# Sparse attention feeding a squared-ReLU layer: the second batch's loads ahead of w_out, first loads by head pair, free PSUM banks, and vector work that yields

## The chip, the cores and the metric

The kernel runs on one core of a Trainium2 chip. A core has five engines with an instruction stream each: TensorE (PE in the profile: matmuls and transposes), VectorE (DVE), ScalarE (ACT), GpSimd (POOL) and SyncE (SP). GpSimd and SyncE also issue the transfers between the device's memory (HBM) and the on-chip buffer (SBUF). Matmul results stand in eight PSUM banks. The metric is the device time of one execution in microseconds (us), as the median over the runs.

## The reference

The inputs q, k and v have 8 batches of 8 heads, 576 positions and 64 dimensions, in fp32. The weights are w_in (512 x 2048) and w_out (2048 x 512).

```
scores = q @ k.T / 8
mask   = heads 0-3: 0 <= i - j < 32          ("local")
         heads 4-7: j <= i and i % 32 == j % 32   ("strided")
attn   = softmax(where(mask, scores, -1e9)) @ v
x      = attn with the heads side by side: 4608 rows of 512
h      = x @ w_in
out    = (s * max(h, 0)**2 + b) @ w_out
```

## The kernel before

**Attention.** A batch is cut into four pairs of heads, m = 0 to 3: two local pairs and two strided ones. q, k and v are loaded and turned to fp16 by the transfer itself (GpSimd's queue), except that the first batch's local v is staged in fp32 by SyncE in the room of w_out (`vl_stage`) and cast by GpSimd. A pair's work (`pair_steps`) is a list of small TensorE steps: transposes of q and k (L405 in the first two batches, L413 after), scores (L533; in the first batch preceded by a matmul that adds the mask, L530), weighted sums with v (L590) and transposes of the result x (L638). Between the steps stand ScalarE's exponentials (L551), VectorE's masks (L559), reciprocals (L605) and scalings (L616), and copies out of PSUM that ScalarE or VectorE may take (L317). The result is xT, the input of the dense layers. In later batches some of the transposes are done by transfers on SyncE's queue.

**Dense layers.** x is cut into nine blocks T of 512 rows. For each block, `ff1` makes 16 x 4 matmuls with w_in (L883), which ScalarE clips at zero (L910; VectorE at L912 for block 0), and a square of two results at a time (L918 on ScalarE, L920 on VectorE) gives gT. For blocks 0 to 2, `ff2` makes 4 x 16 matmuls with w_out (L941), evicted by VectorE (L952). For blocks 3 to 8, `ff2_seven` makes seven products in place of eight from sums of parts of gT (`sums_post`, L723 on VectorE) and of w_out (w_mix), with matmuls at L851 and evictions at L770, L782. The bias needs sums over w_out, made in `bcs_steps` (L968, L979) early in block 0's second layer.

**Order of the work.** Nothing is reordered at run time: each engine runs its stream in order, and waits where an operand isn't there. The streams are written by a planner (`Plan`) when the kernel is built. It keeps a clock `t`, due times `done` for every piece of data, and times `free` for the engines. TensorE's steps are taken from the attention lists or from f1 and f2 as they come due; work of the other engines is posted with `post` (what it needs, its cost by engine, the function that writes it) and written by `flush`, the piece that became ready first being first, on the engine that the plan says ends it first. A step that opens a PSUM bank names a `Group`: a tag (t, s, a, f1 or f2) with one or two banks, taken in strict rotation, so that a step is due only when the bank used `bufs` groups ago was given back. `group_of` chooses the tag by kind and batch, in a fixed rotation over tags for the first batches. While TensorE has nothing due at the start, `keep_running` writes matmuls on constants (L1177).

**Loads.** `load_qk`, `load_s`, `early_v`, `load_vl`, `load_w_in` and `load_w_out` issue on GpSimd, in this order: q, k, strided q, strided k and strided v of batch 0; w_in in three pieces (`weights_in`, after strided q has landed); then `second`. Local q and k have lines ql and kl in the profile, strided ones qs and ks, and v is v_loc and vs. Due times for transfers are figures in the code (`arrive`, `landing`). The core of `second`:

```
weights_out(range(1))
fetch_qk(1)
weights_out(range(1, 4))
load_vl(1)
...
early_v(1)
```

Of the kernel before, what the change touches and what calls it, by code (L numbers as in the profile page):

```python
# [15 lines left out]
class Plan:  # L16
# [6 lines left out]

    LAT = {"A": 70.0, "V": 70.0, "P": 70.0, "D": 12000.0, "X": 7000.0, "Y": 12000.0}

    def __init__(self):
        self.t = 0.0
        self.done = {}
        self.pend = []
        self.free = {"A": 0.0, "V": 0.0, "P": 7000.0, "D": 0.0, "X": 0.0, "Y": 0.0}  # L30
        self.count = {}

    def ready_at(self, needs):
        if any(k not in self.done for k in needs):
# [6 lines left out]
    def flush(self):  # L41
        while True:
            best = None
            for p in self.pend:
                r = self.ready_at(p[0])
                if r is not None and r <= self.t and (best is None or r < best[0]):
                    best = (r, p)
            if best is None:
                return
            r, p = best  # L50
            self.pend.remove(p)
            eng = min(p[1], key=lambda e: max(self.free[e], r) + p[1][e])
            end = max(self.free[eng], r) + p[1][eng]
            self.free[eng] = end
            p[2](eng)
            for k in p[3]:
                if isinstance(k, Group):
                    k = ("rel", k.tag, k.n)
                soon = isinstance(k, tuple) and k[0] == "soon"
                self.done[k] = end + (6000.0 if soon else p[4] or self.LAT[eng])  # L60

    def step_ready(self, s):
        r = self.ready_at(s.needs)
        if r is None:
            return None
        if s.group is not None:
            n = self.count.get(s.group.tag, 0)
            if n >= s.group.bufs:
                k = ("rel", s.group.tag, n - s.group.bufs)
                if k not in self.done:  # L70
                    return None
                r = max(r, self.done[k])
        return r

    def emit(self, s):
        if s.group is not None:
            s.group.n = self.count.get(s.group.tag, 0)
            self.count[s.group.tag] = s.group.n + 1
        s.fn()
        self.t += s.ns  # L80
        for k in s.keys:
            self.done[k] = self.t + 200.0
        for p in s.posts:
            self.post(*p)
        if s.after is not None:
            s.after()

    def next_time(self):

        nxt = [v for v in self.done.values() if v > self.t]  # L90
        assert nxt, "nothing left that could make a step ready"
        return min(nxt)

# [4 lines left out]
class Group:  # L98


    def __init__(self, tag, bufs):
        self.tag, self.bufs, self.n = tag, bufs, None


class Step:
# [6 lines left out]
def kernel(  # L112
# [11 lines left out]
    nc = tc.nc  # L124
# [118 lines left out]
    stage_v(range(2))  # L243
    nc.sync.dma_start(out=negs, in_=h_neg.ap())
    nc.vector.memset(ones16, 1.0)
    nc.vector.memset(part32, 1.0 / 32)
    nc.vector.memset(vl_stage[0:LPAD], 0.0)
    for i in range(2):
        nc.vector.memset(qD_loc[i], 0.0)
        nc.vector.memset(kT_loc[i][:, 0:LPAD], 0.0)  # L250
        nc.vector.memset(qD_str[i], 0.0)
    for i in range(NV):
        nc.vector.memset(v_loc[i][:, :, :, D:D + 1], 1.0)
# [4 lines left out]
    for tl in p_bufs[False]:  # L258
        nc.vector.memset(tl[:, 16 * SQ:], 0.0)

    loaded = {}
    paired = {}

    def load_qk(b):
        for name, src in (("q", q), ("k", k)):
            tl = inp.tile([LQ, NL], FP16, tag=name + "l", name=name + "l")
            loaded[b, name + "l"] = tl
            if b >= (QB_DMA if name == "q" else KB_DMA):

                dst = tl.rearrange("p (m t e d) -> p m e t d", m=2, t=LT, e=2)  # L270
                for h in range(4):
                    nc.gpsimd.dma_start(out=dst[:, h // 2, h % 2],
                                        in_=src[b, h].rearrange("(t p) d -> p t d", p=LQ))
            else:
                nc.gpsimd.dma_start(out=h4(tl), in_=view_l(src, b))
        for name, src in (("q", q), ("k", k)):
            if name == "k":
                ts = ks[b % 2]
            elif b < QS_DMA + 2:
                ts = inp.tile([SR, NS], FP16, tag="qs", name="qs")  # L280
            else:
                ts = loaded[b - 2, "qs"]
            if name == "k" and b in (2, 3) or name == "q" and b in (QS_DMA, QS_DMA + 1):
                nc.gpsimd.memset(ts[64:SR], 0.0)
            load_s(ts, src, b)
            loaded[b, name + "s"] = ts
# [47 lines left out]
    def cast_v(b, loc, mm, key):  # L334
        nt, np_, dst = (LT, 128, v_loc) if loc else (ST, SQ, v_str)

        def g(eng):
            src = vl_stage if loc else loaded[b, "vs"].rearrange(
                "p (h t d) -> p h t d", h=4, d=D)
            for h in range(2 * mm, 2 * mm + 2):  # L340
                copy_on(eng, out=dst[b % NV][0:np_, h, :, 0:D], in_=src[:, h])
        n = nt * D
        plan.post([key], {"P": 1000.0} if loc else {"A": 2 * (170 + 0.83 * n), "V": 540.0}, g,
                  [("cast", b, mm) if loc else ("in", "vs", b, mm)])
        if loc:
            rows_before(b, mm, ("cast", b, mm))

    def rows_before(b, mm, key):
# [5 lines left out]
        def g(eng):  # L354
# [4 lines left out]
    TB, SB, AB, F1B, F2B = 1, 2, 1, 2, 2  # L359
    HEAD_T = 2  # L360
    PE_MASK = 1
    ps = {tag: [psum.tile([128, PS], FP32, name=f"ps_{tag}{i}") for i in range(n)]
          for tag, n in (("t", TB), ("s", SB), ("a", AB), ("f1", F1B), ("f2", F2B))}

    taken = {"a": 0, "t": 0, "s": 0}

    def group_of(kind, b, m, q=False):

        t, a, f1, f2 = ("t", TB), ("a", AB), ("f1", F1B), ("f2", F2B)
        banks = {"a": [a], "t": [t], "s": [("s", SB)]}[kind]  # L370
        if b == 0:
            banks = {"a": [f2, f2, f1], "t": [t, a], "s": [("s", SB), ("s", SB), f1]}[kind]
        elif b == 1 and kind == "a":
            banks = [f1, f1, a]
        elif b >= KB_DMA and kind == "a":
            banks = [a, t]
        elif b == 1 and q:
            banks = [t, f2]
        taken[kind] += 1
        return Group(*banks[taken[kind] % len(banks)])  # L380

    def bank(group):
        return ps[group.tag][group.n % group.bufs]

    def pair_steps(b, m):

# [196 lines left out]
        def av(e, j, group):  # L583
# [13 lines left out]
            if j % per == per - 1:  # L597
# [2 lines left out]
                j0 = j - per + 1  # L600

                def rc(eng):
                    st["rec", e, j] = recp.tile([128, 6, 1], FP32, tag="rec" + group.tag,
                                                bufs=group.bufs, name="rec")
                    nc.vector.reciprocal(out=st["rec", e, j][0:nq, 0:per],  # L605
                                         in_=st["pa", e, j][0:nq, 0:per, D:D + 1])

# [445 lines left out]
    load_qk(0)  # L1053
    early_v(0)
    plan.free["P"] = 7100.0
    for name, at in (("q", 6950.0), ("k", 8750.0)):
        arrive(both(name + "l", 0), at)
    arrive(both("qs", 0), 10100.0)
    arrive(both("ks", 0), 11600.0)
    plan.done["raw", "v", False, 0] = 13800.0  # L1060
    after_landing(0, loaded[0, "ql"][0:1, 0:1])
    stage_v(range(2, 4))
    nc.sync.dma_start(out=masks, in_=h_mask.ap())
    nc.sync.dma_start(out=s_sb, in_=moe_s.to_broadcast([128, 1]))
# [7 lines left out]
        for keys, cost in ([0], 2700), ([1], 2500), ([2, 3], 5000):  # L1072
            arrive([("w_in", c) for c in keys], landing(cost))

    for mm, at in (0, 7100.0), (1, 14400.0):
        plan.done["raw", "v", True, 0, mm] = at
        cast_v(0, True, mm, ("raw", "v", True, 0, mm))
    plan.post([("in", "vl", 0, 0)], {"P": 3300.0}, weights_in, [("w",)])

    def weights_out(chunks):  # L1080
        load_w_out(chunks)
# [2 lines left out]

    def second(eng):

        weights_out(range(1))
        fetch_qk(1)
        weights_out(range(1, 4))
        load_vl(1)  # L1090
        plan.done["raw", "vl", 1] = landing(3200)
        for mm in range(2):
            rows_before(1, mm, ("raw", "vl", 1))
        early_v(1)

    plan.post(both("vl", 0) + both("vs", 0) + [("w",)], {"P": 14000.0}, second, [("free",)])

# [29 lines left out]
    for T in range(NBLK):  # L1127
        if T == 0:

            gr = [Group(*x) for x in (("s", SB), ("s", SB), ("f1", F1B), ("f1", F1B))]  # L1130
            cts = FIRST
            f1 += [ff1(T, ft, ct, gr[ft], cts, True) for ct in cts for ft in range(4)]
        for ft in ff_order(T)[0 if T else 4:]:
            gr = Group("f2", F2B) if T == 0 and ft % 4 < 2 else Group("f1", F1B)
            for ct in range(4):
                f1.append(ff1(T, ft, ct, gr))
        if T == 0:
# [24 lines left out]
    def keep_running(until):  # L1162

        ghz = 1.2 if plan.t < 6000 else 2.4
        n = min(int((until - 100.0 - plan.t) * ghz) - 20, 512) // 128
        for tag, bufs in (("f1", F1B), ("s", SB), ("f2", F2B)):
            k = ("rel", tag, plan.count.get(tag, 0) - bufs)
            if k[2] < 0 or plan.done.get(k, until) <= plan.t:
                break
        else:  # L1170
            return False
        if n < 1:
            return False
        out = ps[tag][plan.count.get(tag, 0) % bufs][:, 0:128 * n]

        def f():
            nc.tensor.matmul(  # L1177
# [90 lines left out]
```

## Time and profile before

| | |
|---|---|
| median of 8 runs (lowest to highest) | 308.95 us (307.92 to 309.71) |
| profiled execution: its time, its span | 307.92 us, 306.1 us |
| TensorE, weight loads | 297.1 us busy (97%), 206.4 us |
| VectorE, ScalarE, GpSimd | 215.9 (71%), 183.5 (60%), 93.2 us (30%) |
| transfers | 37.31 MB, 122 GB/s in the mean |
| granted TensorE clock | 0.998 |

The span runs from the first to the last event of the profiled execution; its own time has 1.8 us more around it. Busy time of an engine is the time in which one of its recorded instructions was running; waits inside a stream are listed apart, with what ended them. A table by stretches gives, for each stretch of time, each engine's busy time with the number of instructions that ran in it (x), then the granted clock, the transfer share and GB/s.

### The profile page before, as it was taken

How to read it: one execution, taken by the hardware profiler on the slowest of the kernel's cores; microseconds unless marked ns; L12 is line 12 of the kernel's file. 1: busy time of each engine (PE TensorE's matmuls, PEld its weight loads, DVE VectorE, ACT ScalarE, POOL GpSimd, SP SyncE). 2: the span in 40 equal slices, each digit the busy share in tenths (PEclk: the TensorE clock that was granted, in tenths of full speed). 3: DMA queues.
4: the chain of work that ended last, by engine and by line, in shares of the span. 5: the costliest groups of instructions: out<-in, count | busy, mean ns of one | idle time of the engine just before them, and what ended most of it. 6: DMA issues, size and time to landing. Idle time of an engine off the chain costs nothing.

```text
span 306.1 us, 6880 instructions
## 1 busy us (share of the span) xinstructions
PE 297.1 (97%) x2686; PEld 206.4 (67%) x2686; DVE 215.9 (71%) x479; ACT 183.5 (60%) x330; POOL 93.2 (30%) x136
## 2 busy tenths in 40 slices
PE   8898999999999999999999999999999999999995
PEld 3764655666655567777567776778888666766884
DVE  6665767799868678449897987688765366737563
ACT  2875856698957795668287945794525444444300
POOL 8561539910880581079105840000000000000000
PEclk9999999999999999999999999999999999999999
DMA  7999999999999999899997999714010200300223
GB/s 128 183 209 207 213 164 169 201 187 149 78 138 184 110 150 109 177 152 135 137 194 132 142 149 188 167 26 133 2 36 35 71 1 34 105 0 2 82 74 121
DMA packets 100796, 37.31 MB, mean 122 GB/s; under 512 B 80875, under 2 KB 97771, under 8 KB 100763
## 3 DMA queue, kind: packets, MB, share of 16 engines
q0 software_dynamic: 57200, 18.08, 59.8%
q1 hardware_dynamic: 43562, 18.78, 31.9%
q8 instruction: 21, 0.34, 0.5%
q14 instruction: 13, 0.10, 0.1%
HBM read 36.86 MB, written 10.32 MB: 154 GB/s over the span
## 4 chain that ended last, share of the span: by engine, by line
PE 87%; DMA 9%; POOL 1%; DVE 1%; issue 1%; ACT 0%; SPq 0%; POOLq 0%
PE ps_f L883 37%; PE ps_f L851 21%; PE ps_f L941 12%; DMA qs<-in_q_dram 5%; PE ps_s L533 5%; PE ps_a L590 3%; DMA w_out_sb<-in_v_dram 2%; DMA ql<-in_q_dram 2%; PE ps_s L851 2%; PE ps_t L413 2%; PE ps_t L590 1%; PE ps_t L851 1%; PE ps_s L941 1%; PE ps_t L638 1%; PE ps_a L851 1%; POOL v_loc L317 1%
## 5 line engine op out<-in xcount | busy, mean ns | idle before, releaser
L883 PE MATMUL ps_f<-xT,w_in_sb 128*128 128x512 f16 (+4 forms) x696 | 148.1, 340 | 0.1
L910 ACT ACTIVATE u<-ps_f 128x512 f16<-128x512 f32 x138 | 81.6, 596 | 73.2 <-PE ps_f L883 71.7
L883 PEld LDWEIGHTS <-w_in_sb 128*128 128x128 f16 x704 | 71.5, 113 | 32.2 <-issue 0.2
L851 PEld LDWEIGHTS <-gT 128*128 128x128 f16 x512 | 49.1, 98 | 11.5
L920 DVE TENSOR_TENSOR gT<-u 128x1024 f16<-128x1024 f16 x50 | 34.3, 687 | 24.6 <-ACT u L910 24.0
L941 PE MATMUL ps_f<-w_out_sb,gT 128*128 128x512 f16 x176 | 47.9, 379 | 0.3 <-DVE gT L920 0.3
L851 PE MATMUL ps_f<-w_out_sb,gT 128*128 128x256 f16 x312 | 43.4, 273 | 0.0
L941 PEld LDWEIGHTS <-gT 128*128 128x128 f16 x192 | 17.2, 98 | 12.3 <-DVE gT L920 0.4
L616 DVE TENSOR_TENSOR x_nat<-ps_a,rec 72x256 f16<-72x256 f32 (+1 forms) x52 | 23.8, 458 | 0.7
L551 ACT ACTIVATE p_loc<-ps_s 128x384 f16<-128x384 f32 x46 | 20.9, 493 | 4.8 <-PE ps_s L533 3.8
L918 ACT ACTIVATE gT<-u 128x1024 f16<-128x1024 f16 x22 | 23.3, 1057 | 0.6
L551 ACT ACTIVATE p_str<-ps_s 72x432 f16<-72x432 f32 (+1 forms) x46 | 20.7, 482 | 1.9 <-PE ps_s L533 1.7
L295 POOL DMA_DIRECT2D v_loc<-in_v_dram x28 | 20.7, 757 | 3.5 <-DMA kl<-in_k_dram 1.4
L590 PEld LDWEIGHTS <-p_str 72*128 72x128 f16 x256 | 15.5, 98 | 9.0 <-issue 1.3
L723 DVE TENSOR_TENSOR gT<-gT 128x1024 f16<-128x1024 f16 x28 | 18.5, 682 | 2.6 <-ACT gT L918 1.3
L851 PE MATMUL ps_f<-w_mix,gT 128*128 128x256 f16 x144 | 18.3, 273 | 0.0
L851 PEld LDWEIGHTS <-S 128*128 128x128 f16 x160 | 15.4, 98 | 3.4
L300 POOL DMA_DIRECT2D v_str<-in_v_dram x16 | 13.1, 823 | 6.7 <-DMA ks<-in_k_dram 2.8
L605 DVE RECIPROCAL rec<-ps_a 72x4 f32<-72x4 f32 (+1 forms) x52 | 9.1, 175 | 8.3 <-PE ps_a L590 8.3
L723 DVE TENSOR_TENSOR S<-gT 128x1024 f16<-128x1024 f16 x16 | 10.6, 686 | 5.6 <-PE ps_f L851 4.5
L1012 POOL COPY gate<-kT 1x1 f16<-1x1 f16 x6 | 1.5, 257 | 40.6 <-DMA kT<-ks 40.6
L851 PE MATMUL ps_f<-w_mix,S 128*128 128x256 f16 x96 | 13.7, 273 | 0.0
(156 smaller groups left out, 417.2 us busy)
## 6 DMA issues: line engine op xcount, KB each, us to landing
out_dram<-o SPq DMA_DIRECT2D x34, 256.0 KB, 2.4
w_out_sb<-in_moe_w_out_dram POOLq DMA_DIRECT2D x4, 512.0 KB, 11.6
v_loc<-in_v_dram POOLq DMA_DIRECT2D x28, 72.0 KB, 7.0
ql<-in_q_dram POOLq DMA_DIRECT2D x6, 288.0 KB, 6.7
qs<-in_q_dram POOLq DMA_DIRECT2D x6, 288.0 KB, 5.8
ks<-in_k_dram POOLq DMA_DIRECT2D x6, 288.0 KB, 7.1
kl<-in_k_dram POOLq DMA_DIRECT2D x4, 288.0 KB, 7.9
kl<-in_k_dram POOLq DMA_DIRECT2D x16, 72.0 KB, 4.2
```

The costliest lines, as they stand in the source:

```text
L295: nc.gpsimd.dma_start(out=vl[LPAD:128, h, :, 0:D], in_=v_band(b, h))
L533: nc.tensor.matmul(out=st["s", g][0:nk, c:c + 2 * nq], lhsT=(st["k"][:, i * nq:i * nq + nk] if loc else st["k"][:, i, 0:SQ]), rhs=st["q"][ ...
L551: nc.scalar.activation(out=st["pw", g][0:nk, 0:2 * n * nq], in_=st["s", g][0:nk, 0:2 * n * nq], func=AF.Exp, scale=scale)
L590: nc.tensor.matmul(out=st["a"][:, j % per, :], lhsT=st["pw", g][0:nk, i * nq:i * nq + WIDE], rhs=vt[0:nk, 2 * mm + e, j, :])
L616: nc.vector.tensor_tensor(out=st["x"][:, j0:j0 + per, 64 * e:64 * e + 64], in0=st["pa", e, j][0:nq, 0:per, 0:D], in1=st["rec", e, j][0:nq, ...
L723: nc.vector.tensor_tensor(out=at(out), in0=at(x), in1=at(y), op=op)
L851: nc.tensor.matmul(out=gts[name, T, t][:, 0] if halves else gts[name, T][:, t], lhsT=lhs(k, t), rhs=rhs(k), start=fresh and k == 0 and (ha ...
L883: nc.tensor.matmul(out=gts["h", T, ft][:, lo:hi], lhsT=w_in_sb[min(ft // 4, 2)][:, ct].rearrange("p (c x l) -> p c l x", x=128, l=4)[:, ma ...
L910: nc.scalar.activation(out=u, in_=gts["h", T, ft], func=AF.Relu)
L918: nc.scalar.activation(out=g, in_=u, func=AF.Square)
L920: nc.vector.tensor_tensor(out=g, in0=u, in1=u, op=ALU.mult)
L941: nc.tensor.matmul(out=gts[id_], lhsT=gts[T][:, ft, ts * 128:(ts + 1) * 128], rhs=w_out_sb[:, ft, cols], start=(ft == 0), stop=(ft == NFT ...
```

## The change

- **Loads.** In `second`, all of batch 1 (q, k, strided q and k, local v, strided v) is issued ahead of the four quarters of w_out. In `load_qk`, local q and k of batch 0 are each issued in two halves, one for each pair of heads: q and k of pair 0, then q and k of pair 1. The due times follow (`AT`), and SyncE's gate waits for the second half of q.
- **Banks.** A `Group` is now a set of named banks, and a step takes the one that the plan says is given back first. The sets for the first batches are wider (for example f2, f1 and a for the weighted sums of batch 0, and t with f1 for q of batch 2). Reciprocals share one tag of eight buffers.
- **Posted work.** `flush` holds back work for VectorE and ScalarE while both are planned more than 800 ns ahead of the clock (`SLACK`), and orders what is ready by its ready time plus an extra: 1500 ns for squares ("g") and sums ("S"), 2500 ns for input casts ("in") and for w_mix.
- **Smaller.** GpSimd may take the cast of batch 0's strided v (at a planned 1500 ns), w_in waits in the plan for strided q, and some of VectorE's first memsets change places.

In the streams as built, TensorE has 12 matmuls fewer of the keep-warm kind (its lines move down by 24: L405 is L429, L883 is L907, L941 is L965), ScalarE has 26 squares in place of 22, and GpSimd has two issues more at the start, two casts of v_str, and three spreads of q in batches 6 and 7.

```diff
+    SLACK = 800.0
+    LATER = {"g": 1500.0, "S": 1500.0, "in": 2500.0, "w_mix": 2500.0}
...
-                if r is not None and r <= self.t and (best is None or r < best[0]):
-                    best = (r, p)
+                if r is None or r > self.t:
+                    continue
+                if p[1].keys() <= {"A", "V"} and min(
+                        self.free[e] for e in p[1]) > self.t + self.SLACK:
+                    continue
+                k = p[3][0]
+                w = r + self.LATER.get(k[0] if isinstance(k, tuple) else None, 0.0)
+                if best is None or w < best[0]:
+                    best = (w, r, p)
...
-            n = self.count.get(s.group.tag, 0)
-            if n >= s.group.bufs:
-                k = ("rel", s.group.tag, n - s.group.bufs)
-                if k not in self.done:
-                    return None
-                r = max(r, self.done[k])
+            free = [self.banks[x] for x in s.group.names if self.banks[x] is not None]
+            if not free:
+                return None
+            r = max(r, min(free))
...
     def load_qk(b):
-        for name, src in (("q", q), ("k", k)):
+        for mm in range(2) if b == 0 else ():
+            hs = slice(2 * mm, 2 * mm + 2)
+            for name, src in (("q", q), ("k", k)):
+                if mm == 0:
+                    loaded[b, name + "l"] = inp.tile([LQ, NL], FP16, tag=name + "l", name=name + "l")
+                nc.gpsimd.dma_start(out=h4(loaded[b, name + "l"])[:, hs],
+                                    in_=view_l(src, b)[:, hs])
+        for name, src in (("q", q), ("k", k)) if b else ():
...
-            banks = {"a": [f2, f2, f1], "t": [t, a], "s": [("s", SB), ("s", SB), f1]}[kind]
+            banks = {"a": f2 + f1 + a, "t": t + a + f2, "s": sc + f1}[kind]
...
     def second(eng):
 
-        weights_out(range(1))
         fetch_qk(1)
-        weights_out(range(1, 4))
         load_vl(1)
         plan.done["raw", "vl", 1] = landing(3200)
         for mm in range(2):
             rows_before(1, mm, ("raw", "vl", 1))
         early_v(1)
+        weights_out(range(4))
```

## The prediction

> **What bounds the kernel now.** I read the page's busy row, then the table by stretches, then TensorE's waits, then GpSimd's issues and waits. The page first, then TensorE's list of waits:
>
> ```profile
> PE 297.1 (97%) x2686; PEld 206.4 (67%) x2686; DVE 215.9 (71%) x479; ACT 183.5 (60%) x330; POOL 93.2 (30%) x136
> GB/s 128 183 209 207 213 164 169 201 187 149 78 138 184 110 150 109 177 152 135 137 194 132 142 149 188 167 26 133 2 36 35 71 1 34 105 0 2 82 74 121
> ```
> ```profile
> PE ps_f L405 <- DMA ql<-in_q_dram: 1.5, 1, 1.5
> PE ps_f L1177 <- DVE w_mix L245: 1.1, 1, 1.1
> PE ps_f L413 <- DMA qs<-in_q_dram: 0.6, 1, 0.6
> ```
>
> TensorE is the bound, but 97% busy overstates it: recorded matmul ends are modelled, and the keep-warm matmuls of L1177 count as busy. So I made a ledger. Every TensorE instruction of the built program, in its order, gets the spacing of two starts in a dense stretch (0.216 us for 512 columns, 0.109 for 256, 0.082 for a 192-column score, 0.065 for a 144-column one, about 0.03 for a 65- to 96-column one, nothing for L1177). All sum to 285 us of work. Counting how many matmuls had started by a time gives the work done; elapsed time minus work is the **lag**:
>
> ```
> us      8    16    22    28    30    34    46    55    85    90   150   300
> work  0.6   5.9  10.1  16.2  16.6  19.4  31.2  39.7  69.3  73.2 133.0 282.8
> lag   7.4  10.1  11.9  11.8  13.4  14.6  14.8  15.4  15.7  16.8  17.0  17.2
> ```
>
> The end is work plus lag plus 3.5 us of last eviction and store. Work is the same in both kernels (285 us; only L1177 drops by 12 instructions). So the change is worth what it takes off the lag: 6.8 us before the first transpose, 5 more up to 22 us (first batch), 2.7 from 28 to 34 (waits for the second batch), 2.4 after 46. The stretches show it: where matmuls are long the count is low anyway, but at 25 to 35 us busy is low too, with DMA at 200 GB/s:
>
> ```profile
> 20.00:25.00 5.00, 4.64 (x32) 2.46 (x30) 1.89 (x8) 2.71 (x8) 0.56 (x1) 1.00 1.13 215
> 25.00:30.00 5.00, 3.77 (x18) 1.75 (x16) 3.03 (x5) 3.37 (x5) 1.11 (x2) 1.00 1.18 203
> 30.00:35.00 5.00, 4.20 (x71) 2.76 (x72) 2.82 (x5) 3.51 (x7) 2.74 (x4) 1.00 1.21 212
> 35.00:40.00 5.00, 5.00 (x57) 3.50 (x56) 4.65 (x9) 4.18 (x11) 1.92 (x3) 1.00 1.05 211
> ```
>
> The timeline of GpSimd shows w_out's first quarter ahead of the second batch's q, and a later issue waiting for the third piece of w_in:
>
> ```profile
> 16.05 0.55 POOL L313 DMA_DIRECT2D w_out_sb<-in_moe_w_out_dram  x1 [0.30 <-POOL v_loc L317]
> 16.58 0.69 POOL L275 DMA_DIRECT2D ql<-in_q_dram  x1
> 26.61 0.56 POOL L313 DMA_DIRECT2D w_out_sb<-in_moe_w_out_dram  x1 [4.70 <-DMA w_in_sb<-in_moe_w_in_dram]
> ```
>
> Issue plus landing time, by issue, gives: w_in's third piece 26.3 (11.7+14.6), w_out's first quarter 28.75 (16.05+12.7), ql 30.2, kl 31.9, qs 33.2, ks 35.1; w_out's others 37.1, 39.8, 43.1; v_loc 43.5 to 45.7; vs 47.9.
>
> **What the skill says.** "DMA: Bandwidth & Descriptors", Queues, rings and completion order: a ring's descriptors are consumed in ring order. The trace agrees: GpSimd's loads land in issue order. So moving a load in GpSimd's stream moves its landing by what no longer stands ahead of it. Its Anatomy of one DMA says that waits happen on the issuing sequencer; here that is GpSimd's 4.70 us before 26.61, for the load eight places back. "Perfetto Trace Analysis", Tensor Engine Instruction, says that TensorE's end times are estimates, which the ledger avoids. "GPSIMD Engine Reference", Elementwise, has GpSimd about twice as slow as VectorE; here a GpSimd cast of 128x384 takes 0.55 us median and VectorE's v_str cast of 72x512 0.25 (0.50 for two).
>
> **Loads of the first batch by head pair.** Two issues more, 2 x 0.69 = 1.4 us of GpSimd. The ring holds q and k until 8.6 us anyway, so qs, ks and vs, issued by 7.4, keep their landings (9.7, 11.3, 13.3). vs itself now waits for the first halves (eight loads back). The first half of q should land at about 5.6 (288 KB took until 6.6 beside v on SP's queue), of k at 6.7, the second halves at 7.7 and 8.7. First scores start after q's copies (2 x 0.64 on ScalarE) and k's (0.64): near 8.0 instead of 9.6. From there ScalarE sets the pace: its list for the batch (6 local exps 2.95, 6 strided 2.9, two copies of kT 1.3, one of qD_str 1.3, three of xT 1.9, three scaled quarters of x_nat 2.8) is 13.1 us; from 7.4 it ends near 20.8, where the last xT copy of before ended at 22.3. **Gain at 22 us: 1.5**, lag 10.3 for 11.9. SP's gate now waits for the second half, so the staged v of heads 2 and 3 lands about 1.1 later, near 15. GpSimd's two added v_str casts (512/384 x 0.55 = 0.73 each, 1.5 in all) run before it, 13.4 to 15, and the local casts follow to 16.9; their AV work runs near 17 in both kernels. Moved memsets cost nothing: part32 is needed only at 50 us, and ScalarE's table load comes earlier.
>
> **Second batch ahead of w_out.** q's issue moves from 16.6 to about 16.9, which costs nothing: the ring is full until 26.3. Without w_out's 2.45 us ahead, ql lands at 27.75, kl 29.4, qs 30.75, ks 32.65. In the new order of TensorE these are needed at work 15.74, 17.61, 18.62 and 20.25. So lag is at least 12.0, 11.8, 12.1, 12.4. The 1.5 us gained at 22 is swallowed by the wait for ql, and the 2.7 us of 28 to 34 becomes about 2: **12.4 at 34 us instead of 14.6**. Then v_loc and vs follow (AV work at 24.85 and 29.49, by 36 and 38 us, early enough at lag 12.4), then w_out. w_out is late next. The bytes up to its end are the same, and the ring ended at 47.9. If that total stands, w_out's quarters land at 39.9, 42.5, 45.2, 47.9; at 205 GB/s without the breaks of 38 to 46 us (164 in the page's row), 2.3 us sooner. They are needed at work 27.02, 29.62, 31.35 (bias sums over three quarters) and 35.06. The third decides: lag 11.6 to 13.9, so 12.4 to 13.9 with the floor above. I take 44.3 us, **lag 13.0 against 14.8: 1.8 us off**. The third batch's loads stand behind w_out: ql near 49, its copy 0.83, against a need at 37.07 + 13 = 50; close, and paid in the range.
>
> **Free banks.** TensorE names one bank's eviction among its waits at 0.4 us (x_nat) and 0.5 (qD_loc), both in the first batch. Worth 0 to 0.9; I take 0, as the load floor lies above it.
>
> **Squares, sums and casts yield.** No instruction is added; four squares move to ScalarE, three of the later q spreads (six copies) to GpSimd, which waits 40.6 us at L1012 anyway. The trace of before cannot show the new order's waits. Lag grows 2.4 after 46 us, 1.1 of it at 85 to 90 where L941 waits for a square behind x_nat on VectorE. The best is all of that gone, 2.4 us. The worst: each of the six last blocks waits one VectorE operation of 0.69 for a square or sum, 4.1 us. I take no change.
>
> **Sum.** 306.1 - 1.8 = 304.3 span; 307.92 - 1.8 = 306.1 for the execution. That one is 1.03 below the median, the lowest of eight; the median goes from 308.95 to 307.1.
>
> **Rivals.**
> - *Later waits shrink too.* For it: VectorE 9.3 and ScalarE 8.8 of 10 us busy at 70 to 80, and the 1.1 us at 86. Against: lag is flat from 95 on. 1.8 + 1 to 2.4 gives 304.7 to 306.2.
> - *Hidden: the same bytes, the same end.* w_out's third quarter at 45.2 or later, and bias sums that wait for it, leave lag 13.9 to 14.6: gain 0.2 to 0.9, 308.1 to 308.8.
> - *Squares too late (slower).* VectorE places a square behind two other operations; L941 and L851 need it first in their blocks. The one instance in the trace cost 1.1 us of lag. Against: sums of blocks from 150 on come in time, lag 17.0 to 17.3. It decides above 1.8 us, three blocks at 0.69; six cost 4.1: 309.3 to 311.
> - *The loads don't move.* Excluded: the built GpSimd stream has w_out's four issues after vs.
>
> **Numbers.** A measurement tells 0.2%, 0.62 us. Load floor as summed (gain 0.9 to 2.6): 0.45. Later waits shrink: 0.23. Hidden: 0.12. Slower: 0.20. So 0.68 faster, 0.12 same, 0.20 slower; the likeliest case alone is 306.3 to 308.0. The range 304.5 to 309.6 leaves a tenth on each side.
>
> **What would show it.** Right: ql waits of L405 (then L429) near 27.7 us instead of 30.2; w_out's landings up to 48; TensorE waiting for w_out near 44; lag 12 to 13 at 46. Wrong: lag at 46 above 14.5, or at 300 more than 3 above its value at 46, with L941 or L851 (L965, L875 after) waiting for gT or S.

## The result, and the profile after

The changed kernel takes **306.03 us** in the median of 11 runs (305.2 to 308.21), the kernel before 308.93 us (32 runs beside it, 307.54 to 309.93). The ratio is 0.992, with a 95% interval of 0.9902 to 0.9938, so the gain by the ratio, which is one of means, is 2.5 us (1.9 to 3.0); the medians are 2.9 us apart. Here and below a ratio leaves out executions that took over 1.5% longer than the fastest of their kernel: one each in experiments 3 (1093.77 us), 7 and 12, three of 14 in experiment 8, four of six in experiment 9. The profiled execution took 306.4 us, of which 304.6 us are the span.

The page's busy row and its row of GB/s over 40 slices of 7.6 us:

```profile
PE 295.4 (97%) x2674; PEld 205.8 (68%) x2674; DVE 216.2 (71%) x474; ACT 184.0 (60%) x330; POOL 99.1 (33%) x146
GB/s 132 194 200 201 139 201 192 180 195 143 88 144 164 118 95 153 124 185 144 125 156 151 156 127 166 195 123 130 15 37 33 71 37 0 105 0 2 69 81 128
```

TensorE is as busy as before, so the busy row says nothing on the gain. The row of GB/s shows something new: the fifth slice (30.5 to 38.1 us) moved 139 GB/s, where the slices on both sides moved 201. TensorE's waits (line, what it waited for: us in total, times, longest):

```profile
PE ps_t L429 <- DMA ql<-in_q_dram: 2.3, 1, 2.3
PE ps_s L1201 <- DVE w_mix L257: 1.1, 1, 1.1
PE ps_f L965 <- DMA w_out_sb<-in_moe_w_out_dram: 0.8, 1, 0.8
PE ps_s L907 <- DMA w_in_sb<-in_moe_w_in_dram: 0.7, 1, 0.7
PE ps_a L429 <- DMA kl<-in_k_dram: 0.5, 1, 0.5
PE ps_f L875 <- DVE o L806: 0.3, 1, 0.3
PE ps_f L429 <- DMA ql<-in_q_dram: 0.2, 1, 0.2
```

The wait for the second batch's q is longer than before, 2.3 us for 1.5, because TensorE comes to it sooner, at 26.6 us instead of 28.7. A wait for w_out is new (0.8 us). Gone are almost all waits for VectorE and ScalarE: without the keep-warm line's wait for w_mix they come to 0.3 us here. Before they came to 2.0 us:

```profile
PE ps_a L405 <- ACT qD_loc L317: 0.5, 1, 0.5
PE ps_s L533 <- DVE kTs L317: 0.4, 1, 0.4
PE ps_a L590 <- DVE x_nat L616: 0.4, 1, 0.4
PE ps_f L1177 <- DVE x_nat L616: 0.4, 1, 0.4
PE ps_f L941 <- DVE gT L920: 0.3, 1, 0.3
```

The stretches (us busy and instructions of PE, PEld, DVE, ACT, POOL, then clock, transfer share, GB/s):

```profile
20.00:25.00 5.00, 4.95 (x24) 2.53 (x23) 2.58 (x5) 2.73 (x5) 0.97 (x2) 1.00 1.14 210
25.00:30.00 5.00, 2.74 (x35) 1.48 (x34) 1.42 (x3) 2.34 (x5) 1.45 (x2) 1.00 1.29 202
30.00:35.00 5.00, 5.00 (x77) 3.53 (x76) 4.72 (x9) 4.92 (x9) 3.66 (x7) 1.00 1.42 118
35.00:40.00 5.00, 5.00 (x44) 3.18 (x43) 4.94 (x7) 4.82 (x11) 4.66 (x6) 1.00 1.06 175
```

From 25 to 30 us TensorE now stands idle for 2.26 us, where it stood for 1.23; from 30 to 35 us it is busy throughout. So the waits of the second batch now stand together, and some of their cost is made up later. The lag (elapsed time less TensorE's work done, as in the prediction) gives the balance:

```
us        8    16    22    28    34    46    55    85    90   150   300
before   7.4  10.1  11.9  11.8  14.6  14.8  15.4  15.7  16.8  17.0  17.2
after    7.1   8.7  10.6  12.3  13.4  14.4  15.3  15.5  15.8  15.7  16.1
```

At 22 us the new kernel is 1.3 us ahead, at 28 us 0.5 behind, at 34 us 1.2 ahead, at 55 us level. What is left of the gain in this execution, 1.1 us at 300 us, comes mostly at 85 to 90 us, where the lag of before grew by 1.1 us and that of after by 0.3. The two profiled executions are 1.5 us apart, the medians 2.9, so a ledger of one execution is good to about a microsecond.

GpSimd's timeline shows what stands ahead of w_out (start, length, line, output, idle time before and what ended it):

```profile
26.64 0.72 POOL L316 DMA_DIRECT2D v_loc<-in_v_dram  x1 [4.27 <-DMA w_in_sb<-in_moe_w_in_dram]
29.09 0.72 POOL L316 DMA_DIRECT2D v_loc<-in_v_dram  x1 [1.73 <-DMA ql<-in_q_dram]
31.08 0.72 POOL L316 DMA_DIRECT2D v_loc<-in_v_dram  x1 [1.26 <-DMA kl<-in_k_dram]
31.87 1.18 POOL L311 DMA_DIRECT2D vs<-in_v_dram  x2
33.24 2.15 POOL L334 DMA_DIRECT2D w_out_sb<-in_moe_w_out_dram  x4 [0.19 <-issue]
```

Each of the first three issues waits until an earlier load has landed, so v's small loads enter the queue one by one, and w_out is issued only at 33.24 us. From 32 to 34 us only 72 GB/s were moved:

```profile
32.00:34.00 2.00, 2.00 (x34) 1.70 (x33) 1.96 (x4) 2.00 (x5) 1.81 (x4) 1.00 1.00 72
```

The transfer share (the second number from the right) is 1.00 all the same, so the profile doesn't tell a queue with too little in it from slow packets.

### The profile page after: what moved, and what is told of

It is laid out like the page before. It is cut to its first block, busy times and chain, and to the rows that moved or that the text cites. A ratio compares the mean times of both kernels' runs of the same rounds, so it can differ in the third digit from the quotient of the medians.

```text
span 304.6 us, 6800 instructions
## 1 busy us (share of the span) xinstructions
PE 295.4 (97%) x2674; PEld 205.8 (68%) x2674; DVE 216.2 (71%) x474; ACT 184.0 (60%) x330; POOL 99.1 (33%) x146
## 4 chain that ended last, share of the span: by engine, by line
PE 83%; DMA 9%; POOL 4%; DVE 2%; issue 1%; ACT 0%; POOLq 0%
PE ps_f L907 36%; PE ps_f L875 20%; PE ps_f L965 13%; DMA kl<-in_k_dram 4%; PE ps_s L557 4%; DMA w_out_sb<-in_moe_w_out_dram 3%; PE ps_a L614 2%; DMA vs<-in_v_dram 2%; PE ps_s L875 2%; PE ps_t L875 1%; PE ps_s L965 1%; PE ps_t L614 1%; PE ps_t L662 1%; PE ps_t L437 1%; PE ps_a L875 1%
## 5 line engine op out<-in xcount | busy, mean ns | idle before, releaser
L907 PE MATMUL ps_f<-xT,w_in_sb 128*128 128x512 f16 (+4 forms) x696 | 148.1, 340 | 0.0
L907 PEld LDWEIGHTS <-w_in_sb 128*128 128x128 f16 x704 | 71.7, 113 | 33.5 <-DMA w_in_sb<-in_moe_w_in_dram 0.8
L875 PEld LDWEIGHTS <-gT 128*128 128x128 f16 x512 | 49.1, 98 | 12.4 <-issue 0.4
L965 PE MATMUL ps_f<-w_out_sb,gT 128*128 128x512 f16 x176 | 47.6, 379 | 0.8 <-DMA w_out_sb<-in_moe_w_out_dram 0.8
L875 PE MATMUL ps_f<-w_out_sb,gT 128*128 128x256 f16 x312 | 44.2, 272 | 0.3 <-DVE o L806 0.3
L944 DVE TENSOR_TENSOR gT<-u 128x1024 f16<-128x1024 f16 x46 | 31.5, 685 | 15.2 <-ACT u L934 14.4
L942 ACT ACTIVATE gT<-u 128x1024 f16<-128x1024 f16 x26 | 27.5, 1057 | 0.7
L640 DVE TENSOR_TENSOR x_nat<-ps_a,rec 72x256 f16<-72x256 f32 (+1 forms) x55 | 25.3, 460 | 0.9
L316 POOL DMA_DIRECT2D v_loc<-in_v_dram x28 | 20.6, 753 | 15.7 <-DMA w_in_sb<-in_moe_w_in_dram 5.7
L965 PEld LDWEIGHTS <-gT 128*128 128x128 f16 x192 | 17.0, 98 | 11.1
L575 ACT ACTIVATE p_loc<-ps_s 128x384 f16<-128x384 f32 x46 | 20.8, 494 | 2.2 <-PE ps_s L557 2.0
L614 PEld LDWEIGHTS <-p_str 72*128 72x128 f16 x256 | 15.2, 98 | 7.3 <-issue 0.2
L875 PE MATMUL ps_f<-w_mix,gT 128*128 128x256 f16 x144 | 19.3, 273 | 0.0
L875 PEld LDWEIGHTS <-S 128*128 128x128 f16 x160 | 15.5, 98 | 3.7
L583 DVE TENSOR_TENSOR p_loc<-p_loc,masks 128x1152 f16<-128x1152 f16 x14 | 10.4, 746 | 8.0 <-ACT p_loc L575 7.9
L875 PE MATMUL ps_f<-w_mix,S 128*128 128x256 f16 x96 | 13.4, 273 | 0.0
L976 DVE SCALAR_TENSOR_TENSOR o<-ps_f,s_sb,bcs 128x512 f32<-128x512 f32 x11 | 8.2, 749 | 6.4 <-PE ps_f L965 6.2
```

The source lines that it names most:

```text
L316: nc.gpsimd.dma_start(out=vl[LPAD:128, h, :, 0:D], in_=v_band(b, h))
L575: nc.scalar.activation(out=st["pw", g][0:nk, 0:2 * n * nq], in_=st["s", g][0:nk, 0:2 * n * nq], func=AF.Exp, scale=scale)
L614: nc.tensor.matmul(out=st["a"][:, j % per, :], lhsT=st["pw", g][0:nk, i * nq:i * nq + WIDE], rhs=vt[0:nk, 2 * mm + e, j, :])
L640: nc.vector.tensor_tensor(out=st["x"][:, j0:j0 + per, 64 * e:64 * e + 64], in0=st["pa", e, j][0:nq, 0:per, 0:D], in1=st["rec", e, j][0:nq, ...
L875: nc.tensor.matmul(out=gts[name, T, t][:, 0] if halves else gts[name, T][:, t], lhsT=lhs(k, t), rhs=rhs(k), start=fresh and k == 0 and (ha ...
L907: nc.tensor.matmul(out=gts["h", T, ft][:, lo:hi], lhsT=w_in_sb[min(ft // 4, 2)][:, ct].rearrange("p (c x l) -> p c l x", x=128, l=4)[:, ma ...
```

## The experiments

Every kernel ran beside the kernel before on one chip; ratios are to that kernel. Each edit of the program makes the planner write new streams unless said otherwise. So the first group undoes parts with new plans, the second keeps the streams and changes transfers alone, the third crosses the parts, and the last two ask single questions.

**1. The old order of loads.** In `second`, w_out's first quarter stands again ahead of batch 1:

```diff
     def second(eng):
+        weights_out(range(1))
         fetch_qk(1)
+        weights_out(range(1, 4))
         load_vl(1)
...
-        weights_out(range(4))
```

> The changed kernel with one edit undone: in second, w_out's first quarter is again issued ahead of batch 1's q and k and the other three ahead of its v, as before the change. Load theory (the prediction's: the order of loads is worth 1.8 us): slower than the changed kernel by 1.5 to 2, near 307.8 us, with lag near 14.6 at 34 us and 14.8 at 46. Rival, later waits (in the profiled pair lag is equal at 55 us, 15.3 in both, and the gain lies after 85 us): within 0.5 us of the changed kernel, near 306.0; lag at 34 back at 14.6, but lag at 55 still near 15.3 and at 150 near 15.7.

Measured: 1.0129 (1.009 to 1.0168), median 312.59 us. That is 6.5 us behind the changed kernel, more than either theory gave. After the keep-warm line's wait, TensorE's list for it has:

```profile
PE ps_s L557 <- DMA kT_alt<-kl: 1.0, 1, 1.0
PE ps_f L965 <- DVE gT L944: 0.9, 1, 0.9
```

Its lag is 12.8 us at 46, 1.6 less than after, and then grows to 17.7 at 150 and 19.3 at 300. So in this execution the loss lies not in the stage of the loads but in later blocks. It can't be read as the price of the order; the plan changed with it (experiment 5 holds it still). The profiled execution was also the fastest of six (310.22 us), so 2.4 us of the distance from the median aren't in this trace; four of the six show a mean granted clock of 0.989 to 0.995.

**2. No yielding.**

```diff
-    SLACK = 800.0
-    LATER = {"g": 1500.0, "S": 1500.0, "in": 2500.0, "w_mix": 2500.0}
+    SLACK = 1e12
+    LATER = {}
```

> The changed kernel with posted work written as before the change: nothing is held back and nothing is put behind by an extra (SLACK very large, LATER empty). Loads, halves and banks stay. Load theory: no difference, 305.5 to 306.5 us. Rival, later waits: slower by 1 to 1.5 us, near 307.2, with lag equal to the changed kernel's up to 46 us (14.4) and 1 us or more above it at 150 (15.7).

Measured: 0.9889 (0.9864 to 0.9913), median 304.99 us (304.66 to 305.93). The changed kernel is faster without its yielding, by 1.0 us, but the two intervals overlap by 0.1%. About half of that goes with the clock: three of the changed kernel's twelve executions show a mean granted clock of 0.988 to 0.994, none of these six is under 0.999, and without those three the distance is 0.5 us. The lag is 13.4 at 46 and 14.3 at 90: the stall of 85 to 90 us is gone here too. So it was not the yielding that removed it.

**3. The first loads whole.** Local q and k of batch 0 in one load each, with the due times and SyncE's gate of the kernel before:

```diff
-        for mm in range(2) if b == 0 else ():
+        for mm in ():
...
-        for name, src in (("q", q), ("k", k)) if b else ():
+        for name, src in (("q", q), ("k", k)):
...
-    AT = {"ql0": 5700.0, "kl0": 6800.0, "ql1": 7900.0, "kl1": 8900.0, "qs": 10100.0,
+    AT = {"ql0": 6950.0, "kl0": 8750.0, "ql1": 6950.0, "kl1": 8750.0, "qs": 10100.0,
```

> The changed kernel with batch 0's local q and k loaded whole again (two issues, due times of before, SyncE's gate on the first element). Load theory: the first batch ends 1.3 us later (lag 11.9 at 22 us for 10.6), but TensorE waits for batch 1's q until 28.8 us in both, so lag at 29 is 13.1 to 13.5 and the time is that of the changed kernel within 0.4. Rival, the early start is worth what it gains: slower by 1.3 us, near 307.3, lag at 34 near 14.7 for 13.4.

Measured: 1.0007 (0.9988 to 1.0025), 2.7 us behind the changed kernel. The lag at 22 is 12.4, 1.8 more than after, but at 34 it is 13.8 for 13.4. The profiled executions are 1.4 us apart, and most of that arises between 46 us (14.9 for 14.4) and 85 us (17.1 for 15.5), not in the first batch. Again the new plan is mixed in; experiment 6 takes it out. This kernel has the new order and free banks, and is no faster than the kernel before.

**4. The old rotation of banks.**

```diff
-            banks = {"a": f2 + f1 + a, "t": t + a + f2, "s": sc + f1}[kind]
+            banks = {"a": [f2, f2, f1], "t": [t, a], "s": [sc, sc, f1]}[kind]
...
+        taken[kind] += 1
+        banks = banks[taken[kind] % len(banks)]
...
-            gr = [Group("s", SB, "f1", F1B) for _ in range(4)]
+            gr = [Group(*x) for x in (("s", SB), ("s", SB), ("f1", F1B), ("f1", F1B))]
```

(and the other sets of `group_of` and `ff1` likewise). The rotation over tags is back; within a tag of two banks the one given back first is still taken.

> The changed kernel with the choice of PSUM bank as before the change (one tag for each step, in the fixed rotation over tags, and block 0's clipped results on their old tags; within a tag of two banks the one given back first). Load theory and later waits by vector order: no difference beyond 0.5 us. Rival, free banks carry the gain: slower by 1 us or more, with TensorE or the planner's order losing it in the first 60 us (lag at 55 above 16).

Measured: 1.0061 (1.0036 to 1.0086), median 310.75 us, 4.4 us behind the changed kernel and slower than before. TensorE's waits have entries of a kind that the changed kernel doesn't have. Lines from its list:

```profile
PE ps_f L614 <- DVE u L936: 1.0, 1, 1.0
...
PE ps_f L965 <- ACT u L934: 0.8, 1, 0.8
PE ps_s L557 <- ACT kT_loc L338: 0.7, 1, 0.7
PE ps_t L437 <- ACT qD_loc L338: 0.6, 1, 0.6
```

L614 multiplies p_loc with v_loc and needs no u: it waited for VectorE to evict another result from the bank that it was to write. L965 with `ACT u` and L437 with `ACT qD_loc` are of the same kind; L557 needs kT_loc itself. All waits for VectorE and ScalarE come to 4.3 us here, to 0.3 us after. The largest fall at 9.0, 40.6 and 42.9 us. The lag at 46 is 17.3 for 14.4: 2.9 of the 3.5 us by which the two spans differ. The plan is new here too, so these bank waits are what the old rotation cost in this plan.

**5. The order alone, all other streams held.** GpSimd issues w_out's first quarter ahead of batch 1's q and k; the instructions of the other engines are those of the changed kernel:

```diff
     def second(eng):
+        load_w_out(range(1))
         fetch_qk(1)
...
-        weights_out(range(4))
+        load_w_out(range(1, 4))
+        for c in range(4):
+            arrive([("w_out", c)], landing(2400 if c < 3 else 3000))
```

> The changed kernel's streams of TensorE, VectorE, ScalarE and SyncE, instruction for instruction; only GpSimd issues w_out's first quarter ahead of batch 1's q and k again (the planner's due times stay those of the changed kernel). Direct theory (the load floor of the prediction): batch 1's q lands near 30.2 us, TensorE waits for it, lag at 34 rises to 14.5 or more (13.4 in the changed kernel's profile), the wait for w_out near 41 goes; slower than the changed kernel by 0.5 to 1.5 us, 306.5 to 307.5. Rival, re-planning (what the edit to the loads brings is mostly that the planner writes other streams, as the 6.5 us of the run with the old order suggest): within 0.4 us of the changed kernel.

Measured: 1.0024 (1.0006 to 1.0042), 3.2 us behind the changed kernel. From TensorE's waits, and three stretches of 2 us:

```profile
PE ps_t L429 <- DMA ql<-in_q_dram: 4.2, 1, 4.2
...
PE ps_a L429 <- DMA kl<-in_k_dram: 0.9, 1, 0.9
```
```profile
30.00:32.00 2.00, 0.79 (x25) 0.67 (x26) 0.00 (x0) 0.30 (x1) 1.27 (x2) 0.92 1.28 204
32.00:34.00 2.00, 2.00 (x7) 0.68 (x6) 1.62 (x3) 1.96 (x3) 0.91 (x2) 0.50 1.47 188
34.00:36.00 2.00, 2.00 (x31) 1.09 (x30) 1.01 (x2) 0.70 (x2) 1.18 (x2) 0.73 2.18 128
```

q lands at 31.2 us instead of 28.8, and the wait grows by 1.9 us. Then comes something that no theory had: after 4.2 us without a matmul, the granted clock (the third number from the right) was 0.50 and then 0.73, with 0.92 in the stretch ahead. That is up to 2 x (0.08 + 0.50 + 0.27) = 1.7 us of TensorE time lost. So up to half of the 3.2 us is the clock, and the rest later data. The other executions agree: in 20 of 21 the mean granted clock was 0.989 to 0.994, where 0.994 of 307 us leaves 1.8 us out. The plan of the kernel before had more matmuls to put there, and its wait of 1.5 us left the clock at 1.00.

**6. The first loads whole, all other streams held.** Experiment 3's loads and gate, with `AT` as in the changed kernel, so that the plan stays.

> The changed kernel's streams of TensorE, VectorE, ScalarE and SyncE, instruction for instruction; only GpSimd loads batch 0's local q and k whole (two issues in place of four). Direct theory (the load floor swallows the first batch's gain): first scores 1 to 1.5 us later, lag at 22 near 11.9, lag at 34 as in the changed kernel, time within 0.4 us of it, 305.6 to 306.4; then the 2.7 us of the run with whole loads came from its other streams. Rival, the early start itself carries through: 307.3 or more.

Measured: 0.9941 (0.9921 to 0.996), 0.6 us behind the changed kernel with overlapping intervals. The lag at 22 is 12.9 for 10.6; at 34 it is 13.8 for 13.4, and at 46 equal, 14.4. What the halves bring in the first batch, the wait for q of the second takes away. By difference, some 2 of experiment 3's 2.7 us belong to the plan.

**7. Neither yielding nor the new order; 8. neither yielding nor free banks.** Each combines the edit of experiment 2 with that of 1 or 4.

> The changed kernel without yielding (SLACK very large, LATER empty) and with the old order of loads in second, planned anew. If the order of the loads is worth its direct effect only: 0.5 to 2 us slower than the changed kernel without yielding (305.0), so 305.5 to 307. If the old order is bad by itself in any plan: 6 us slower, near 311.

> The changed kernel without yielding and with the old choice of banks, planned anew. If free banks carry the gain in any plan: 3 us or more slower than the changed kernel without yielding (305.0), so 308 or more, with lag at 55 above 16. If the 4.7 us of the run with old banks came from how that plan fell out with yielding: 305 to 306.5.

Measured: 0.9976 (0.9961 to 0.9991) for the old order, and 1.0032 (1.0007 to 1.0057) for the old banks. Against experiment 2 the banks are worth 4.4 us, as with yielding, and the order 2.7 us, where it was 6.5 with yielding. (The profiled execution of 8 took 316.45 us, where the median is 309.41, so its trace isn't read.)

**9. The kernel before with the new order alone.** In `second` of the kernel before, the same move as in the change, and nothing else.

> The kernel before with one part of the change: the new order of loads in second (all of batch 1, then w_out), planned anew with the old banks, whole loads and the old order of posted work. Load theory as predicted (the order of loads alone lowers the lag at 34 to 46 us by about 2): 306.5 to 307.5 us. Interlock theory (with the old banks TensorE's plan cannot use the earlier loads: with new loads and old banks lag at 46 was 17.3, with both old 14.8): no faster than before, 308.5 to 311, lag at 46 of 15 or more.

Measured: 1.008 (1.0052 to 1.0108), so this is slower than before, by 2.5 us. It rests on two executions, 310.96 and 311.58 us; the other four took 315.66 to 317.59. From TensorE's waits (the first line is that for q):

```profile
PE ps_f L405 <- DMA ql<-in_q_dram: 1.3, 1, 1.3
...
PE ps_f L883 <- ACT u L910: 0.9, 2, 0.7
PE ps_s L941 <- ACT p_loc L551: 0.8, 1, 0.8
PE ps_f L590 <- DVE x_nat L616: 0.8, 1, 0.8
...
PE ps_s L533 <- DVE o L952: 0.7, 1, 0.7
```

None of these last four lines reads what it waited for: a score at L533 doesn't use the output o, nor a product at L941 the p_loc of an attention batch. They waited for banks, 3.2 us together: 0.8 us at 43 us, the rest between 67 and 85 us. The second batch's q came at 28.1 us instead of 30.2, as the change means it to, and the banks were then not to be had in the order of the strict rotation.

**10. The kernel before with free banks**, the change's smaller edits with them; old order, whole loads, no yielding.

> Free banks and the small edits alone: the changed kernel without yielding, with the old order of loads and whole loads of batch 0, planned anew. If free banks are worth 4.5 us in any setting: 304 to 305. Interlock theory (banks pay only with the earlier loads): 307.5 to 308.7, near the kernel before.

Measured: 1.0053 (1.0031 to 1.0076), slower than before by 1.6 us. One wait stands out in its list:

```profile
PE ps_f L907 <- ACT u L934: 2.2, 1, 2.2
```

L907 doesn't read u either; with free banks too, a plan can put a step on a bank that is late in fact. (The profiled execution took 311.46 us, where the median is 309.81, so not every execution need have this wait in full.) Banks without the new order bring nothing here.

**11. One quarter of w_out early.** Experiment 2's kernel, with w_out's first quarter issued between batch 1's strided k and its v, the other three last. It was to fill the stretch with little traffic:

```diff
         fetch_qk(1)
+        weights_out(range(1))
         load_vl(1)
...
-        weights_out(range(4))
+        weights_out(range(1, 4))
```

> The changed kernel without yielding, with w_out's first quarter issued after batch 1's strided k and ahead of its v (the other three last), planned anew. Ring theory (GpSimd's wait for the load eight back leaves the ring nearly empty at 32 to 38 us, 72 to 187 GB/s, and w_out ends 1 us later for it): no dip at 32 to 34 us, w_out's first quarter near 36 instead of 41, lag at 46 near 12.5 instead of 13.4, 304 to 304.6 us. Rival: batch 1's v comes 2.5 us later and takes it back, 305 or more.

Measured: 0.9875 (0.9856 to 0.9894), median 304.84 us. The stretch is filled:

```profile
32.00:34.00 2.00, 2.00 (x33) 1.64 (x32) 1.74 (x4) 1.99 (x5) 1.51 (x4) 1.00 1.26 197
```

197 GB/s, where the changed kernel had 72 and experiment 2 had 133 in the same two microseconds. The first quarter is there at 35.9 us instead of 41.5 and the last at 47.3 instead of 48.9, and no wait for w_out is in TensorE's list. But experiment 2 has none either; the lag at 46 is 14.0, no better than experiment 2's 13.4, and the time is the same as experiment 2's within the intervals. So what was left of the dip in experiment 2 cost nothing that can be measured. This kernel is faster than the changed kernel too: its interval lies wholly under that one's.

**12. Holding back alone** (`SLACK` of 800 kept, `LATER` empty).

> The changed kernel with LATER empty and SLACK kept: work is held back while both engines are full, but squares, sums and casts have no extra. If the extra is what costs the 1 us between the changed kernel (306.0) and the one without yielding (305.0): 304.7 to 305.4. If holding back costs it: 305.8 to 306.5 or more.

Measured: 0.9944 (0.9915 to 0.9972), runs from 304.81 to 309.19 us. That is 1.7 us above experiment 2, with intervals that just don't overlap, and level with the changed kernel. So the extra for squares, sums and casts isn't needed for the loss. That holding back as such costs it isn't shown: the profiled execution, the fastest at 304.81 us, has experiment 2's lag from 46 us to the end, so the loss lies in the spread of the executions, which one trace doesn't explain. The extra alone wasn't run.

**Put together** (ratio to before; "halves" means the first loads by head pair):

```
                         old order, old banks   new, old     old, free    new, free
whole loads, no yield        1                  1.008 (9)    1.0053 (10)  not run
whole loads, yield           not run            not run      not run      1.0007 (3)
halves, no yield             not run            1.0032 (8)   0.9976 (7)   0.9889 (2)
halves, yield                not run            1.0061 (4)   1.0129 (1)   0.992 (after)
plan of after held: order undone (5) 1.0024, whole loads (6) 0.9941
```

With new order and halves, old banks cost 4.4 us, with yielding or without. With free banks and halves, the old order costs 2.7 or 6.5. Yielding costs 1.0, 0.9 and, with the old order, 4.7 us. No kernel with only one of the two, new order or free banks, gains more than 0.24%; every gain above that has both. Both aren't enough: experiment 3 has them, planned anew with whole loads, and gains nothing. No row has all four corners, and outside the last line every number has its own plan in it. So that order and banks pay together fits all runs, but it isn't separated from the luck of the plans.

## Why the prediction was right, and where it wasn't

The time was forecast at 307.1 us and is 306.03; a gain of 1.8 was summed, and 2.5 measured. That the sum is this near is in part luck, for its terms were wrong in both directions. The whole 1.8 us was to be there at 46 us, where the two profiled executions are 0.4 us apart; most of the rest came at 85 to 90 us, which the prediction left as it was. Of the signs that were named, lag of 12 to 13 at 46 didn't come (14.4, just under the 14.5 that was to mean wrong). The upper bound of the gain, 2.6, should be 2.4 by its own terms, lag 12.4 for 14.8.

- **First batch: right.** First scores were put at 8.0 us, and start at 8.00; the last copy of xT was put at 20.8, and ended at 20.6; lag at 22 was put at 10.3, and was 10.6. That all this is swallowed by the wait for ql was forecast too, and experiment 6 shows it. A term was mis-sized without harm: GpSimd's two v_str casts took 1.23 us together, not 1.5.
- **Second batch's q: right, within what one execution tells.** Forecast to land at 27.75; it landed at 28.8 in the profiled execution, and at 27.3 in experiment 2, with the same issues. Lag at 34 was put at 12.4, and was 13.4 and 12.0. The last load, ks, was put at 32.65, and landed at 32.7.
- **w_out late next: right in kind, too early in the figures.** The first quarter was put at 39.9 at the latest and the end at 47.9; they landed at 41.5 and 48.9. The step "the bytes up to its end are the same" left out that little is moved just ahead of w_out; where that stretch was filled, the end was 47.3 (experiment 11). The wait of 0.8 us at 41 is for the first quarter, not for the third at 44. So lag at 46 came to 14.4, not 13.0. The rival *Hidden* had 13.9 to 14.6 there and so was right at this place, and wrong on the end.
- **Later stall: the rival *Later waits shrink too* was right on the end.** Growth after 46 was taken as unchanged at 2.4 us, and was 1.7. Its reason was wrong: experiment 2 hasn't the stall of 85 to 90 us either, without any yielding. The wait for gT there (L941, later L965) is in the traces of all four plans for the old order (before 0.3 us, experiments 1 and 10 0.9, 7 0.2) and in none for the new order. So it went with the plan for the new order.
- **Failed step: free banks taken at 0 (bounds 0 to 0.9).** I read the 0.4 and 0.5 us bank waits of the trace before as the most that banks could be worth. That trace shows what banks cost at the old arrival of data and in its own plan. With the new order and halves the old rotation over tags costs 4.4 us (experiments 4 and 8, each planned anew), and the order alone is slower than before (9). The order, taken at 1.8 us, is worth 3.2 with the streams held (5), of which up to 1.7 is the clock. In these runs the two don't add up: with halves and no yielding one stands at -0.24% (7), the other at +0.32% (8), both together at -1.1% (2). The corner with neither wasn't run.
- **Yielding taken at 0: not refuted.** The kernel is 1.0 us faster without it (experiment 2), with intervals that overlap, and half of that goes with three executions of lower clock. The slower rival named squares that come late; in the changed kernel no wait of L965 or L875 for gT or S is in TensorE's list, so that mechanism wasn't at work. How yielding costs, if it does, is not settled: no wait in the list of the changed kernel answers to it.

Open stays why experiments 1 and 10 lose most of their time after 55 us. Both have the stall of 85 to 90 us, and later blocks wait for single things, up to 1.0 and 2.2 us. Since each edit rewrites all streams after it, and experiment 1's order with held streams costs 3.2 us but planned anew 6.5, I hold the plan to be the cause; that is argued, not shown.

## What to carry to other kernels

A load that comes earlier may pay only if the work that it feeds gets its buffers earlier too: price the order of loads and the rotation of banks together, since a trace shows bank waits only for the arrivals that it had. Where a planner writes the streams, hold them still and change one transfer (experiments 5 and 6) to get the direct price, for new plans alone moved the time by 2 to 3 us here. And count work done against elapsed time: TensorE was at 97% in both kernels.

## What was not expected of the hardware

- A wait of 4.2 us on TensorE brought the granted clock to 0.50 afterwards; the wait of 2.3 us in the changed kernel left it at 1.00. "TensorE: Matmul & The Clock Gate" in the Trainium skill, What's actually happening, gives an idle window of about 3.4 us for this; the two traces agree. The wait of 4.2 us so cost its delay and up to 1.7 us more. Some executions of the changed kernel may pay this too: three of its twelve show a mean clock of 0.988 to 0.994, against three of 111 of the kernel before; that its q wait does this isn't shown, since only one execution was traced.
- Identical streams don't repeat to the microsecond, and in these runs the spread goes with the plan: on one chip, 33 executions of the kernel before took 307.36 to 309.41 us and 22 of experiment 10 took 308.6 to 313.06.
- A copy of 72x512 to fp16 took GpSimd 0.62 us, little more than the 0.55 us of a 128x384 one.
